# Attention and two mixture layers on one core: maxima over partitions by TensorE products instead of GpSimd's all-reduce, mask and identity by VectorE instead of GpSimd's select

## The chip, the cores and the metric

The kernel runs on one core of a Trainium2 chip. The time is device microseconds (us) of one execution, from its first to its last instruction and the little that lies around them; a comparison takes the median of several executions of each kernel on the same chip. A core has five engines with a queue of their own, each worked off in order: TensorE (PE, with its weight loads, PEld), VectorE (DVE), ScalarE (ACT), GpSimd (POOL) and SyncE (SP, which issues the transfers).

## The reference

Three layers follow each other; the inputs of the second layer's weights are float64, all others float32.

```python
# 1. attention, q, k, v: (2, 8, 576, 64); sm_attn: softmax(q k^T / 8) v
out_d = sm_attn(mean4(q), mean4(k), mean4(v))       # 144 pooled positions
out_up = np.repeat(out_d, 4, axis=2)
scores = np.where(np.abs(i - j) < 4, q @ k.T / 8, -1e9)
x = out_up + softmax(scores) @ v                    # -> (1152, 512)
# 2. gated layer, w_gate, w_val: (512, 1536), w_out: (1536, 512)
g = x @ w_gate
x = (g * sigmoid(g) * (x @ w_val)) @ w_out
# 3. eight experts, w1: (8, 512, 1024), w2: (8, 1024, 512)
logits = x @ w_gate2
P = np.exp(logits - logits.max())
for _ in range(8):
    P /= P.sum(1, keepdims=True) + 1e-09
    P /= P.sum(0, keepdims=True) + 1e-09
    P *= N / E
out = sum(P[:, e:e+1] * (np.maximum(x @ w1[e], 0) @ w2[e]) for e in range(8))
```

## The kernel before, in words

**Attention.** The 16 heads go in 8 pairs. Of a pair, `pooled` (L326) adds groups of four columns: k on VectorE (`kd`), q on GpSimd (`qt`, `qd`), and `pooled_v` (L338) the same of v on GpSimd (`vt`, `vdz`). `scores` (L347) puts the mask into PSUM by a product of `identb` and `maskb` (L352), adds q k^T for five windows of 128 keys (L355, L359) and the pooled scores (L361); VectorE takes the maxima (`stm`, `nb`), ScalarE the exponentials (`ex`), and GpSimd divides by the sums (L384 to L388). `turn` (L391) transposes the result on TensorE with `ident` (L397 to L401), and `combine` (L408) multiplies by v (L417, L425). In the same time the first column blocks of the second layer are made ready and multiplied.

**Second layer.** The weights come as words of float64, are put together into float32 by ACT and DVE (`load_f64`, L162, tiles `raw` and `cv`), and split into a high and a low half of 16 bits (`split`, L143): ACT writes the high half (L147), DVE the low one (L148). A product is three products of halves (`mm3`, L150, all on L155). The halves need a scale, a power of two from the largest magnitude of the operand: per partition from an ACT or DVE pass, then over the partitions by `allmax` (L138), then four DVE instructions on a column (`pow2`, L129 to L132: `u`, `u`, `s`, `i`). There are twelve column blocks f; tokens go in two chunks c, of 512 (c = 0) and 640 (c = 1). `prep_gv` makes block f ready, `gv_step` multiplies it (`gv`), and chunk 1 follows chunk 0 by three blocks. Blocks 0 to 2 of chunk 0 run beside the attention.

**Third layer.** The operands of the seven products of Winograd's form of Strassen's method (`p`, `h_step` L671), then the second product (`y`, `y_step` L721), for one expert after the other; weights come by `prep_w1` and `prep_w2`. The routing (`routing`, L596) has eight iterations: row sums on DVE (`rs`), and a product of `ones` and `prob` on TensorE (L612) for column sums, read by DVE (`cs`, L613 to L617).

**What sets the order.** Each engine's queue is laid down in advance by a scheduler that simulates the program; the code's own order, priorities and waits are its input. In the queue nothing overtakes.

**Where `allmax` is used.** 34 places: the bound on x1 (`v`), the twelve blocks (`gv`), two chunks of the second layer's product (`a`), two of its output (`x2`), the logits (`lg`), and `w1` and `w2` of eight experts. Before, it is one GpSimd instruction,

```python
        G.partition_all_reduce(g, mx, channels=P, reduce_op=RED.max)      # L140
```

one to twelve columns wide; where there is more than one column, the caller reduces them by DVE behind it. The mask of the band, the identity and `ones` are made at the start by GpSimd (L98 to L117); ACT copies `ident` to `identb` and `mask` to `maskb`.

Of the kernel before, what the change touches and what calls it, by code (L numbers as in the profile page):

```python
# [8 lines left out]
F32 = mybir.dt.float32  # L9
F16 = mybir.dt.float16  # L10
BF16 = mybir.dt.bfloat16
# [5 lines left out]
RED = bass_isa.ReduceOp  # L17
# [38 lines left out]
def tile_kernel(ctx, tc, qT, kT, vw, vd4, va, wgv, wo, wg2, w1, w2, out):  # L56
# [14 lines left out]

    def tmp(n, nm):
        return wp.tile([P, 16], F32, tag="tmp", bufs=56, name=nm)[:, :n]

# [1 line left out]
    # products of zeros while the first loads run, so that the tensor engine's clock is up  # L76
# [10 lines left out]
    V.memset(qz[0][64:, 0], 0.0)  # L87
    V.memset(qz[0][:64, 1], 0.0)
    V.memset(qz[1][64:, 0], 0.0)
# [3 lines left out]
    for i in range(2):  # L93
# [3 lines left out]
    mask = ap.tile([P, P], F32, tag="mask", bufs=1, name="mask")  # L97
    G.memset(mask, 0.0)  # L98
    G.affine_select(out=mask, in_=mask, compare_op=ALU.is_ge, fill=NEG, base=FAC - 1,
                    pattern=[[-1, P]], channel_multiplier=1)  # L100
    band = G.affine_select(out=mask, in_=mask, compare_op=ALU.is_ge, fill=NEG, base=FAC - 1,
                    pattern=[[1, P]], channel_multiplier=-1)
    with tc.issue_after(band.ins):
        ident = ap.tile([P, P], F32, tag="ident", bufs=1, name="ident")
        make_identity(nc, ident)
        identb = ap.tile([P, P], BF16, tag="identb", bufs=1, name="identb")
        A.copy(identb, ident)
        maskb = ap.tile([P, 4, P], BF16, tag="maskb", bufs=1, name="maskb")
        A.copy(maskb, mask[:, None, :].to_broadcast([P, 4, P]))
        G.memset(qz[1][:64, 1], 0.0)  # L110
        for i in range(2):
            G.memset(vz[i][:, :, 0, 64:], 0.0)
            G.memset(vz[i][:, :, 1, :64], 0.0)
            G.memset(vdz[i][:, :, 0, 64:], 0.0)
            G.memset(vdz[i][:, :, 1, :64], 0.0)
        ones = cp.tile([P, P], F32, name="ones")
        G.memset(ones, 1.0)  # L117
# [20 lines left out]
    def allmax(mx, n, nm):  # L138
        g = tmp(n, f"g_{nm}")
        G.partition_all_reduce(g, mx, channels=P, reduce_op=RED.max)  # L140
        return g
# [20 lines left out]
    def load_f64(src, nm, relu):  # L162
        """float64 words -> float32, by moving sign, exponent and mantissa.

        The high words, read as float32, order like the float64s; up to HI_MIN lie magnitudes below float32's
        normal range, whose exponents must not wrap: they become zeros."""
        raw = wp.tile([P, 2 * DM, 2], U32, tag="raw", bufs=2, name=f"raw{nm}")
        nc.sync.dma_start(raw.rearrange("p n w -> p (n w)"), src.bitcast(U32))
        f = mp.tile([P, 2 * DM], F32, tag="cv", bufs=2, name=f"cv{nm}")
        o, lo, hi = f.bitcast(U32), raw[:, :, 0], raw[:, :, 1]  # L170
        h = hi.bitcast(F32)
        if relu:
            A.activation(f, h, AF.Relu, scale=-1.0)
# [38 lines left out]
    def prep_w1(e):  # L212
        """The left operands of the seven products, of one column block of each half at a time."""
# [8 lines left out]
        m = tmp(1, f"mw1{e}")  # L222
        V.tensor_reduce(m, allmax(mx, 4, f"w1{e}"), axis=AX.X, op=ALU.max)
        s, inv = pow2(m, 1, f"w1{e}", room=4.0)
# [25 lines left out]
    def prep_w2(e):  # L250
# [10 lines left out]
        m = tmp(1, f"mw2{e}")  # L261
        V.tensor_reduce(m, allmax(mx, 4, f"w2{e}"), axis=AX.X, op=ALU.max)
        s, inv = pow2(m, 1, f"w2{e}")
# [55 lines left out]
    def attention():  # L319
        """Generator: the pieces of the attention, of two heads at a time."""  # L320
# [153 lines left out]
    def gv_step(c, f, early):  # L474
# [17 lines left out]
        if early:  # L492
            # silu(g) = g (1 + tanh(g / 2)) / 2, in the table that holds exp
# [30 lines left out]
    def act_split(c):  # L524
# [3 lines left out]
        g = allmax(sc, KF1, f"a{c}")  # L528
        m = tmp(1, f"ma{c}")
        V.tensor_reduce(m, g, axis=AX.X, op=ALU.max)  # L530
        s, ia[c] = pow2(m, 1, f"a{c}")
# [16 lines left out]
    def w_out(c):  # L548
        """x2, its part of the routing's logits, and the right operands of the seven products."""
# [18 lines left out]
    def operands(c, x2, mx):  # L568
        o, nh = CH[c]
        pool = m2 if c else mp  # L570
        m = tmp(1, f"m2{c}")
        V.tensor_reduce(m, allmax(mx, KD, f"x2{c}"), axis=AX.X, op=ALU.max)
        s, ix2[c] = pow2(m, 1, f"x2{c}", room=4.0)
# [22 lines left out]
    def routing():  # L596
# [4 lines left out]
        g = allmax(m, 1, "lg")  # L601
        V.tensor_scalar(g, g, -1.0, None, op0=ALU.mult)
# [3 lines left out]
        for it in range(8):  # L606
# [4 lines left out]
            ps = psr.tile([P, 512], F32, tag="rt", name=f"cs{it}")  # L611
# [37 lines left out]
    psr = ctx.enter_context(tc.tile_pool(name="psr", bufs=1, space=PSUM, reuse_waits="tile"))  # L649
    psm = ctxP.enter_context(tc.tile_pool(name="psm", bufs=2, space=PSUM, reuse_waits="tile"))  # L650
# [9 lines left out]
    lgps = psr.tile([P, 512], F32, tag="rt", name="lgps")[:, :TT * KD * E]  # L660
    lgps = lgps.rearrange("p (t d e) -> p t d e", t=TT, d=KD)
# [9 lines left out]
    def h_step(e, c, between=None):  # L671
        """relu(w1^T x2) by Winograd's form of Strassen's seven products, on halves of rows, columns and k."""
# [141 lines left out]
```

## Time and profile before

| | us |
|---|---|
| median of 3 runs | 1089.38 |
| lowest and highest | 1088.95, 1089.58 |
| span of the profiled execution | 1088.1 |
| PE busy in it | 1022.6 (94%) |
| DVE, ACT, POOL busy | 763.4, 449.8, 96.7 |
| mean granted clock of TensorE | 0.975 |

The span of the profiled execution runs from its first to its last instruction; the median of the runs is 1.3 us above it. The profile's page gives busy time by engine and, in forty slices of 27.2 us, the busy share in tenths. Granted clock 1.00 is TensorE's full speed (2.4 GHz), 0.5 its lower level (1.2 GHz). The attention fills the first 176 us; from there on TensorE works almost without a gap.

### The profile page before, as it was taken

The page shows a single profiled execution, that of the slowest core. Times are in us where ns is not written, and L with a number is a line of the kernel's source. Part 1 is how long each engine was busy: PE and PEld are TensorE (multiplying, and loading weights), DVE is VectorE, ACT ScalarE, POOL GpSimd, SP SyncE. Part 2 cuts the span into 40 slices and gives each one's busy share as a digit, 9 for nine tenths or more (in the row PEclk, how much of TensorE's full clock was granted, in tenths as well). Part 3 has the DMA queues.
Part 4 walks back from the last instruction along what each step waited for, and adds up shares of the span by engine and source line. Part 5 has one row for each costly group of instructions (what it writes and reads, how often), then busy time and mean ns, then how long its engine had stood idle before and what let it go on. Part 6 is the DMA issues. An engine that isn't in the chain of part 4 may idle for free.

```text
span 1088.1 us, 16397 instructions
## 1 busy us (share of the span) xinstructions
PE 1022.6 (94%) x6493; PEld 657.3 (60%) x6493; DVE 763.4 (70%) x1557; ACT 449.8 (41%) x933; POOL 96.7 (9%) x147
## 2 busy tenths in 40 slices
PE   5756677999999999999999999999999999999998
PEld 4745455566656776656666565575665665666654
DVE  5835565788768299979758866984974974985631
ACT  4654364666646073723414422621541441351210
POOL 3634440000000020000000000000000000000000
PEclk9977888999999999999999999999999999999999
DMA  7721222243202002210301201211111030120001
GB/s 200 243 68 33 85 91 78 86 147 116 79 1 78 1 2 78 78 42 37 117 1 39 86 31 39 78 40 39 65 52 33 8 117 1 40 78 1 1 35 53
DMA packets 23613, 67.92 MB, mean 62 GB/s; under 512 B 12208, under 2 KB 12464, under 8 KB 17136
## 3 DMA queue, kind: packets, MB, share of 16 engines
q1 hardware_dynamic: 23536, 66.87, 18.2%
q8 instruction: 51, 0.84, 0.3%
q14 instruction: 26, 0.21, 0.1%
HBM read 64.50 MB, written 2.36 MB: 61 GB/s over the span
## 4 chain that ended last, share of the span: by engine, by line
PE 83%; DVE 6%; issue 6%; POOL 2%; ACT 2%; POOLq 0%; ACTq 0%; DVEq 0%
PE y L155 34%; PE p L155 29%; PE gv L155 9%; PE wo L155 6%; PE o L425 1%; PE lgps L546 1%; PE s L355 1%; PE s L361 0%; DVE nb L370 0%; DVE cvg L174 0%; ACT ex L373 0%; POOL ex L384 0%; DVE gv L148 0%; DVE stm L365 0%; POOL g_gv L140 0%
## 5 line engine op out<-in xcount | busy, mean ns | idle before, releaser
L155 PE MATMUL y<-w,hhl 128*128 128x512 f16 (+1 forms) x1752 | 396.2, 376 | 0.0
L155 PE MATMUL p<-bop,w 128*128 128x320 f16 (+1 forms) x2688 | 353.8, 286 | 0.8 <-DVE u L685 0.7
L155 PEld LDWEIGHTS <-w 128*128 128x128 f16 x2688 | 263.0, 98 | 90.5 <-issue 1.3
L155 PEld LDWEIGHTS <-hhl 128*128 128x128 f16 x1752 | 171.5, 98 | 178.0
L155 PE MATMUL gv<-xhl,gv 128*128 128x320 f16 (+1 forms) x864 | 148.9, 333 | 5.7 <-DVE act L504 4.0
L713 ACT ACTIVATE hhl<-h 128x640 f16<-128x640 f32 (+1 forms) x128 | 83.1, 676 | 169.0 <-DVE h L685 169.0
L155 PEld LDWEIGHTS <-gv 128*128 128x128 f16 x864 | 85.5, 99 | 63.1 <-issue 12.5
L744 DVE SCALAR_TENSOR_TENSOR acc<-y,pe,acc 128x512 f32<-128x512 f32 (+1 forms) x64 | 47.3, 739 | 101.3 <-PE y L155 100.5
L147 ACT ACTIVATE w<-r,s_w 128x256 f16<-128x256 f32 (+1 forms) x96 | 71.0, 783 | 110.2 <-PE y L155 86.3
L714 DVE SCALAR_TENSOR_TENSOR hhl<-h,hhl 128x640 f16<-128x640 f32 (+1 forms) x128 | 94.3, 753 | 15.9 <-ACT hhl L713 14.7
L685 DVE SCALAR_TENSOR_TENSOR h<-p,u 128x256 f32<-128x256 f32 (+1 forms) x192 | 84.8, 452 | 19.0 <-PE p L155 13.3
L148 DVE SCALAR_TENSOR_TENSOR w<-r,s_w,w 128x256 f16<-128x256 f32 (+1 forms) x96 | 78.2, 833 | 16.7 <-ACT w L147 16.7
L155 PE MATMUL wo<-ahl,wo 128*128 128x320 f16 (+1 forms) x432 | 71.5, 326 | 0.0
L685 DVE SCALAR_TENSOR_TENSOR u<-p,u 128x320 f32<-128x320 f32 (+1 forms) x128 | 57.3, 448 | 4.8 <-PE p L155 4.1
L147 ACT ACTIVATE w<-cmb,s_w 128x512 f16<-128x512 f32 x64 | 43.0, 710 | 41.1 <-DVE cmb L238 38.9
L155 PEld LDWEIGHTS <-wo 128*128 128x128 f16 x432 | 42.3, 99 | 26.9
L140 POOL PARTITION_ALL_REDUCE g_w<-mxw x16 | 7.3, 458 | 567.1 <-DVE mxw L136 331.8
L702 ACT ACTIVATE s<-p 128x256 f32<-128x256 f32 (+1 forms) x64 | 25.4, 397 | 53.3 <-PE p L155 53.3
L136 DVE TENSOR_REDUCE mxw<-r 128x1 f32<-128x1024 f32 x32 | 37.5, 1213 | 14.1 <-DMA r<-in_w 14.1
L148 DVE SCALAR_TENSOR_TENSOR w<-cmb,s_w,w 128x512 f16<-128x512 f32 x64 | 45.9, 741 | 0.0
L258 ACT ACTIVATE j<-r 128x1024 f16<-128x1024 f32 x32 | 33.4, 1046 | 25.4 <-DMA r<-in_w 25.4
L373 ACT ACTIVATE ex<-s,nb 128x128 f32<-128x128 f32 x64 | 22.6, 372 | 24.7 <-DVE nb L367 24.2
(192 smaller groups left out, 956.2 us busy)
## 6 DMA issues: line engine op xcount, KB each, us to landing
r<-in_w SPq DMA_DIRECT2D x32, 1024.0 KB, 4.8
rawg<-in_wgv SPq DMA_DIRECT2D x12, 1024.0 KB, 5.1
rawo<-in_wo SPq DMA_DIRECT2D x6, 1024.0 KB, 4.9
vz<-in_vw SPq DMA_DIRECT2D x16, 160.0 KB, 4.6
k<-in_kT SPq DMA_DIRECT2D x8, 288.0 KB, 6.7
qz<-in_qT SPq DMA_DIRECT2D x16, 144.0 KB, 4.0
v<-in_vd SPq DMA_DIRECT2D x8, 288.0 KB
va<-in_va SPq DMA_DIRECT2D x8, 288.0 KB, 7.9
```

The lines of the kernel that those rows point to most:

```text
L136: V.tensor_reduce(o, i, axis=axis, op=ALU.max, apply_absolute_value=True)
L147: return (A.activation(hi, src, AF.Copy, scale=s), V.scalar_tensor_tensor(lo, src, s, hi, op0=ALU.mult, op1=ALU.subtract))
L148: V.scalar_tensor_tensor(lo, src, s, hi, op0=ALU.mult, op1=ALU.subtract))
L155: T.matmul(ps, lhsT=wf(i, k), rhs=xf(j, k), start=n == 0, stop=n == 3 * nk - 1)
L258: A.activation(junk, t[:, 2 * j:2 * j + 2].rearrange("p a n -> p (a n)"), AF.Abs, accum_out=mx[:, 2 * i + j:2 * i + j + 1])
L355: T.matmul(ps[0][:, w * P:(w + 1) * P], lhsT=q[:, j, ws], rhs=k[:, ws], start=False, stop=w == NW - 2)
L373: A.activation(ex[:, 0, w * P:(w + 1) * P], ps[0][:, w * P:(w + 1) * P], AF.Exp, scale=0.125, bias=nb[:, w:w + 1], accum_out=sm[:, w:w + 1])
L685: V.scalar_tensor_tensor(o, ps, HSC, u, op0=ALU.mult, op1=ALU.add)
L702: A.activation(s1, p1, AF.Copy, scale=HSC)
L713: ra = A.activation(t[:, 0], h, AF.Relu)
L714: rv = V.scalar_tensor_tensor(t[:, 1], h, 0.0, t[:, 0], op0=ALU.max, op1=ALU.subtract)
L744: V.scalar_tensor_tensor(acc[t][:, ds], ps, p[:, t:t + 1], acc[t][:, ds], op0=ALU.mult, op1=ALU.add)
```

## The change

`allmax` becomes: a DVE maximum over the columns where there are several, a product with the identity that turns the column into a row in one partition of PSUM, a DVE maximum along that row, and a product of a row of ones with the one number, which puts it into all partitions; the four instructions of `pow2` read it in PSUM. The piece of PSUM comes from `small`: during the attention a buffer of the two that the early blocks' `gv` products use (tag `y`), afterwards one tile `rt` that lives to the end, whose bank also holds the logits and the routing's column sums. The mask and the identity come from arithmetic on a table of column minus row that DVE builds. GpSimd clears the `qz` tiles. Comments went too; lines move by up to 11.

```diff
+    def small(nm):
+        if routed:
+            return routed[0][:, TT * KD * E:]
+        return psg.tile([P, 512], F32, tag="y", name=f"sm_{nm}")
...
-    mask = ap.tile([P, P], F32, tag="mask", bufs=1, name="mask")
-    G.memset(mask, 0.0)
-    G.affine_select(out=mask, in_=mask, compare_op=ALU.is_ge, fill=NEG, base=FAC - 1,
-                    pattern=[[-1, P]], channel_multiplier=1)
...
-        make_identity(nc, ident)
-        A.copy(identb, ident)
-        A.copy(maskb, mask[:, None, :].to_broadcast([P, 4, P]))
...
+    V.memset(dist[:, 0:1], 0.0)
+    for n in (1, 2, 4, 8, 16, 32, 64):
+        V.tensor_scalar(dist[:, n:2 * n], dist[:, :n], float(n), None, op0=ALU.add)
+    V.transpose(row, dist[:, :32])
+    for n in range(32, P, 32):
+        V.tensor_scalar(row[n:n + 32, 0:1], row[n:n + 32, 0:1], float(n), None, op0=ALU.add)
+    V.tensor_scalar(dist, dist, row[:, 0:1], None, op0=ALU.subtract)
+    V.tensor_tensor(dist, dist, dist, op=ALU.mult)
+    V.tensor_scalar(identb, dist, 0.0, None, op0=ALU.is_equal)
+    V.tensor_scalar(maskb, dist[:, None, :].to_broadcast([P, 4, P]), FAC * FAC - 0.5, NEG,
+                    op0=ALU.is_ge, op1=ALU.mult)
+    V.tensor_scalar(ident, dist, 0.0, None, op0=ALU.is_equal)
...
     def allmax(mx, n, nm):
-        g = tmp(n, f"g_{nm}")
-        G.partition_all_reduce(g, mx, channels=P, reduce_op=RED.max)
-        return g
+        if n > 1:
+            m = tmp(1, f"gm_{nm}")
+            V.tensor_reduce(m, mx, axis=AX.X, op=ALU.max)
+            mx = m
+        ps = small(nm)
+        r = tmp(1, f"gr_{nm}")
+        T.matmul(ps[:1, :P], lhsT=mx, rhs=ident, start=True, stop=True)
+        V.tensor_reduce(r[:1], ps[:1, :P], axis=AX.X, op=ALU.max)
+        T.matmul(ps[:, P:P + 1], lhsT=ones[:1], rhs=r[:1], start=True, stop=True)
+        return ps[:, P:P + 1]
...
-            ps = psr.tile([P, 512], F32, tag="rt", name=f"cs{it}")
+            ps = routed[0]
```

The order of POOL's queue in the attention, third pair's scaling (`ex`) and fifth pair's sums. `ISA` stands for a custom instruction: of each two rows of L140 the first sets up the engine's code and the second is the all-reduce, and the one of L334 sets it up again for the ordinary operations. Before:

```order
L384 TENSOR_TENSOR ex_606<-ex_606,rs_614 128x512
L386 TENSOR_SCALAR ex_606<-ex_606,rs_614 128x128
L388 TENSOR_TENSOR ex_606<-ex_606,rs_614 72x288
L140 ISA
L140 ISA g_gv_479<-mxg_477 128x1
L334 ISA
L334 TENSOR_TENSOR qd_827<-qt_830 128x288
```

and now:

```order
L399 TENSOR_TENSOR ex_617<-ex_617,rs_625 128x512
L401 TENSOR_SCALAR ex_617<-ex_617,rs_625 128x128
L403 TENSOR_TENSOR ex_617<-ex_617,rs_625 72x288
L360 TENSOR_TENSOR vdz_85<-vt_955 72x2x64
L348 TENSOR_TENSOR qt_978<-qz_81 128x576
```

No custom instruction stands between them any more; over the whole queue one is left, ahead of the first `vt`.

The order of PE's queue where block 6 of the second layer begins (`mxg`: a block's maxima by partition, `gr`: the number, `gv_1639` and `gv_1665`: block 6's weights). Before:

```order
L155 MATMUL gv_2_1_1834<-xhl,gv_1317 128x320
L155 LDWEIGHTS gv_1639
L155 MATMUL gv_6_0_1911<-xhl,gv_1639 128x512
L155 LDWEIGHTS gv_1639
L155 MATMUL gv_6_0_1911<-xhl,gv_1639 128x512
```

and now:

```order
L174 MATMUL gv_2_1_1864<-xhl,gv_1331 128x320
L157 MATMUL rt<-ident,mxg_1674 1x128
L159 MATMUL rt<-gr_gv_1676,ones 128x1
L157 MATMUL rt<-ident,mxg_1788 1x128
L159 MATMUL rt<-gr_gv_1790,ones 128x1
L174 LDWEIGHTS gv_1665
L174 MATMUL gv_6_0_1943<-xhl,gv_1665 128x512
```

The four products of blocks 6 and 7 stand directly ahead of the first product that needs block 6's scale; it is the same at blocks 10 and 11.

The order of PE's queue at the routing's fourth column sums, around the end of the first expert's `p` products and the start of its `y` products. Before:

```order
L155 MATMUL y_0_0_4305<-w_0_3_3958,hhl_0_7_3908 128x512
L612 MATMUL cs_3636<-prob,ones 128x72
L155 LDWEIGHTS hhl_0_2_3831
L155 MATMUL y_1_0_4332<-w_0_1_3952,hhl_0_2_3831 128x512
```

and now:

```order
L174 MATMUL p_1_27_4263<-bop_3550,w_0_11_2984 128x320
L622 MATMUL rt<-prob,ones 128x72 x5
L157 MATMUL rt<-ident,gm_w_3980 1x128
L159 MATMUL rt<-gr_w_3982,ones 128x1
L174 LDWEIGHTS hhl_0_0_3625
L174 MATMUL y_0_0_4351<-w_0_0_3993,hhl_0_0_3625 128x512
```

Before, the eight column sums lie among products, 50 to 120 `p` or `y` products apart, and the `y` products begin while `p` products are left. Now the first three are spread, and the last five follow each other without a product between them, with the two of `w2`'s maximum behind them and the first `y` product, which needs the scale from it, behind those. On DVE the reduces and divisions of these iterations follow each other in the same way.

## Rows read from the trace of the kernel before

**Rows 1.** The page: busy time by engine; PE's busy tenths and the granted clock in tenths, both in 40 slices of 27.2 us; and one of the costliest groups, with busy us and mean ns.

```profile
PE 1022.6 (94%) x6493; PEld 657.3 (60%) x6493; DVE 763.4 (70%) x1557; ACT 449.8 (41%) x933; POOL 96.7 (9%) x147
...
PE   5756677999999999999999999999999999999998
...
PEclk9977888999999999999999999999999999999999
...
L714 DVE SCALAR_TENSOR_TENSOR hhl<-h,hhl 128x640 f16<-128x640 f32 (+1 forms) x128 | 94.3, 753 | 15.9 <-ACT hhl L713 14.7
```

**Rows 2.** Busy time by stretch: start:end, length, then PE, PEld, DVE, ACT, POOL busy (instructions), granted clock, the transfers' busy share and GB/s.

```profile
0.00:176.00 176.00, 114.92 (x740) 93.73 (x741) 102.79 (x228) 85.95 (x320) 75.70 (x115) 0.84 0.38 111
13.50:49.00 35.50, 32.51 (x251) 30.25 (x252) 29.44 (x65) 23.84 (x114) 24.14 (x35) 0.95 0.76 233
49.00:176.00 127.00, 80.10 (x486) 62.91 (x485) 67.22 (x150) 59.92 (x204) 48.10 (x64) 0.80 0.22 65
405.00:430.00 25.00, 25.00 (x168) 16.33 (x166) 24.76 (x59) 11.94 (x20) 0.39 (x1) 1.00 0.25 85
488.60:576.40 87.80, 87.80 (x554) 54.03 (x553) 64.83 (x126) 31.59 (x53) 0.74 (x2) 1.00 0.14 49
```

**Rows 3.** The chain of waits that ended last: first its shares in 45 to 180 us (135 us), then pieces of it in order of time (start, length, what). "issue" is time in which the engine waited for nothing the profile shows. The row at 52.73 is the longest such piece; 49.37 and 162.60 are the first and the last of eleven such pieces of over 1 us, 43.8 us together, that lie at GpSimd's all-reduces.

```profile
by line: issue 37.8%; PE o L425 6.2%; PE gv L155 5.1%; DVE nb L370 3.6%; POOL ex L384 3.1%; PE o L417 2.4%; DVE stm L365 2.3%; PE s L361 2.2%; ACT ex L373 2.2%; POOL qd L334 2.1%; DVE cvg L174 1.7%; DVE cvg L179 1.7%; POOL qt L333 1.7%; DVE
...
49.37 2.91 issue
...
52.73 8.64 issue
...
162.60 5.53 issue
...
176.31 3.88 PE gv L155 x18
```

**Rows 4.** GpSimd in order of time: start, length, line, operation; in brackets the idle time before it and what ended it.

```profile
10.37 0.28 POOL L99 TENSOR_SCALAR_AFFINE_SELECT mask<-mask 128x128 f32<-128x128 f32 x1 [9.45 <-issue]
...
52.28 0.38 POOL L140 PARTITION_ALL_REDUCE g_v<-mxv  x1 [6.34 <-issue]
...
61.37 1.14 POOL L333 TENSOR_TENSOR qt<-qz 128x576 f32<-128x576 f32 x1 [8.71 <-issue]
...
76.36 0.38 POOL L140 PARTITION_ALL_REDUCE g_gv<-mxg  x1 [5.97 <-issue]
...
83.58 0.65 POOL L334 TENSOR_TENSOR qd<-qt 128x288 f32<-128x288 f32 x1 [6.84 <-issue]
```

**Rows 5.** Who waited for whom in 13.5 to 176 us: total us, times, longest.

```profile
DVE u_gv L129 <- POOL g_gv L140: 35.1, 5, 9.6
...
PE s L352 <- ACT identb L107: 10.0, 1, 10.0
```

**Rows 6.** TensorE, transposes of a head's scores (`turn`), four to a row: the first head, the fourth, the sixteenth and last.

```profile
25.81 0.60 PE L397 MATMUL t<-ident,ex 128*128 128x128 f32 x4
...
38.80 0.60 PE L397 MATMUL t<-ident,ex 128*128 128x128 f32 x4
...
161.69 0.60 PE L397 MATMUL t<-ident,ex 128*128 128x128 f32 x4
```

**Rows 7.** The chain of waits at the routing: TensorE's smallest float32 products, the logits' with 8 columns (three products) and column sums with 72 (one product). A float32 product is two records.

```profile
382.52 0.57 PE lgps L546 x6
...
410.36 0.17 PE cs L612 x2
```

**Rows 8.** TensorE in order of time, 36 to 45 us: start, length (the last one's modelled end included), records. L359 is one float32 product of 128 columns; the eight records of L355 stand there twice, behind work and behind a gap.

```profile
36.62 1.05 PE L355 MATMUL s<-k,qz 128*128 128x128 f32 x8
...
38.04 0.44 PE L359 MATMUL s<-k,qz 128*128 128x128 f32 x2
38.32 0.65 PE L309 MATMUL vv<-va 128*128 128x128 bf16 x5
...
42.74 0.47 PE L352 MATMUL s<-maskb,identb 128*128 128x512 bf16 x1 [2.98 <-DVE x L431]
43.00 1.91 PE L355 MATMUL s<-k,qz 128*128 128x128 f32 x8
```

**Rows 9.** VectorE in order of time: the first and the last of five small instructions of one routing iteration that follow each other.

```profile
407.02 0.22 DVE L617 TENSOR_TENSOR prob<-prob,cs 128x72 f32<-128x72 f32 x1
...
408.00 0.23 DVE L610 TENSOR_TENSOR prob<-prob,rs 128x72 f32<-128x72 f32 x1
```

**Rows 10.** VectorE, one instruction of `pow2` over the third layer: 15 of them, busy us, mean ns.

```profile
L129 DVE TENSOR_SCALAR u_w<-mw 128x1 f32<-128x1 f32 x15 | 2.2, 149 | 0.2
```

**Rows 11.** The split of a block's 1024 columns in order of time: the high half on ACT, the low one (of a later block) on DVE.

```profile
191.08 1.13 ACT L147 ACTIVATE gv<-cvg,s_gv 128x1024 f16<-128x1024 f32 x1
...
208.02 1.28 DVE L148 SCALAR_TENSOR_TENSOR gv<-cvg,s_gv,gv 128x1024 f16<-128x1024 f32 x1 [1.21 <-ACT gv L147]
```

**Rows 12.** The tail of a block of the second layer: ACT's pass over `gv`, DVE's `act`.

```profile
184.83 0.79 ACT L514 ACTIVATE act<-gv,iv 128x640 f32<-128x640 f32 x1 [1.18 <-PE gv L155]
...
188.14 0.88 DVE L515 SCALAR_TENSOR_TENSOR act<-gv,iv,act 128x640 f32<-128x640 f32 x1 [5.25 <-issue]
```

**Rows 13.** VectorE, the same instruction of four columns, alone and while GpSimd works.

```profile
22.85 0.15 DVE L370 TENSOR_TENSOR nb<-stm,scl 128x4 f32<-128x4 f32 x1
...
66.51 2.95 DVE L370 TENSOR_TENSOR nb<-stm,scl 128x4 f32<-128x4 f32 x1
```

More of the change, by code (lines that the diff above doesn't have):

```diff
@@ L4 @@
 import concourse.tile as tile
-from concourse import bass_isa, mybir
+from concourse import mybir
 from concourse._compat import with_exitstack
-from concourse.masks import make_identity
 F32 = mybir.dt.float32
@@ L16 @@
 PSUM = bass.MemoryType.PSUM
-RED = bass_isa.ReduceOp
 B, H, S, D = 2, 8, 576, 64
@@ L70, in ps_mm @@
         return psm.tile([P, 2, 512], F32, tag="mm", name=nm)
+    def small(nm):
+        if routed:
+            return routed[0][:, TT * KD * E:]
+        return psg.tile([P, 512], F32, tag="y", name=f"sm_{nm}")
+    routed = []
     def tmp(n, nm):
@@ L86, in tile_kernel @@
     sts = [ap.tile([P, 8], F32, tag=f"sts{i}", bufs=1, name=f"sts{i}") for i in range(2)]
-    V.memset(qz[0][64:, 0], 0.0)
-    V.memset(qz[0][:64, 1], 0.0)
-    V.memset(qz[1][64:, 0], 0.0)
+    for i in range(2):
+        G.memset(qz[i][64:, 0], 0.0)
+        G.memset(qz[i][:64, 1], 0.0)
     scl = ap.tile([P, 8], F32, tag="scl", bufs=1, name="scl")
@@ L95, in tile_kernel @@
         V.memset(sts[i], 1.0)
-    mask = ap.tile([P, P], F32, tag="mask", bufs=1, name="mask")
-    G.memset(mask, 0.0)
-    G.affine_select(out=mask, in_=mask, compare_op=ALU.is_ge, fill=NEG, base=FAC - 1,
-                    pattern=[[-1, P]], channel_multiplier=1)
[L101 to L104, printed above, removed]
-        make_identity(nc, ident)
-        identb = ap.tile([P, P], BF16, tag="identb", bufs=1, name="identb")
-        A.copy(identb, ident)
-        maskb = ap.tile([P, 4, P], BF16, tag="maskb", bufs=1, name="maskb")
-        A.copy(maskb, mask[:, None, :].to_broadcast([P, 4, P]))
[L110 to L117, printed above, removed]
+    for i in range(2):
+        G.memset(vz[i][:, :, 0, 64:], 0.0)
+        G.memset(vz[i][:, :, 1, :64], 0.0)
+        G.memset(vdz[i][:, :, 0, 64:], 0.0)
+        G.memset(vdz[i][:, :, 1, :64], 0.0)
@@ new lines, in tile_kernel @@
+    ones = cp.tile([P, P], F32, name="ones")
+    G.memset(ones, 1.0)
+    dist = ap.tile([P, P], F32, tag="dist", bufs=1, name="dist")
+    V.memset(dist[:, 0:1], 0.0)
+    for n in (1, 2, 4, 8, 16, 32, 64):
+        V.tensor_scalar(dist[:, n:2 * n], dist[:, :n], float(n), None, op0=ALU.add)
+    row = ap.tile([P, 32], F32, tag="row", bufs=1, name="row")
+    V.transpose(row, dist[:, :32])
+    for n in range(32, P, 32):
+        V.tensor_scalar(row[n:n + 32, 0:1], row[n:n + 32, 0:1], float(n), None, op0=ALU.add)
@@ new lines, in tile_kernel @@
+    V.tensor_scalar(dist, dist, row[:, 0:1], None, op0=ALU.subtract)
+    V.tensor_tensor(dist, dist, dist, op=ALU.mult)
+    identb = ap.tile([P, P], BF16, tag="identb", bufs=1, name="identb")
+    V.tensor_scalar(identb, dist, 0.0, None, op0=ALU.is_equal)
+    maskb = ap.tile([P, 4, P], BF16, tag="maskb", bufs=1, name="maskb")
+    V.tensor_scalar(maskb, dist[:, None, :].to_broadcast([P, 4, P]), FAC * FAC - 0.5, NEG,
+                    op0=ALU.is_ge, op1=ALU.mult)
+    ident = cp.tile([P, P], F32, name="ident")
@@ L221, in prep_w1 @@
             r.append(t)
-        m = tmp(1, f"mw1{e}")
-        V.tensor_reduce(m, allmax(mx, 4, f"w1{e}"), axis=AX.X, op=ALU.max)
-        s, inv = pow2(m, 1, f"w1{e}", room=4.0)
+        s, inv = pow2(allmax(mx, 4, f"w1{e}"), 1, f"w1{e}", room=4.0)
         a = []
@@ L260, in prep_w2 @@
             r.append(t)
-        m = tmp(1, f"mw2{e}")
-        V.tensor_reduce(m, allmax(mx, 4, f"w2{e}"), axis=AX.X, op=ALU.max)
-        s, inv = pow2(m, 1, f"w2{e}")
+        s, inv = pow2(allmax(mx, 4, f"w2{e}"), 1, f"w2{e}")
         b = []
@@ L527, in act_split @@
         V.tensor_tensor(sc, amx[c], wo_inv, op=ALU.mult)
[L528 to L531, printed above, removed]
+        s, ia[c] = pow2(allmax(sc, KF1, f"a{c}"), 1, f"a{c}")
         V.tensor_scalar(sc, wo_inv, s, None, op0=ALU.mult)
@@ L570, in operands @@
         pool = m2 if c else mp
-        m = tmp(1, f"m2{c}")
-        V.tensor_reduce(m, allmax(mx, KD, f"x2{c}"), axis=AX.X, op=ALU.max)
-        s, ix2[c] = pow2(m, 1, f"x2{c}", room=4.0)
+        s, ix2[c] = pow2(allmax(mx, KD, f"x2{c}"), 1, f"x2{c}", room=4.0)
         w = xp.tile([P, 7, 2, 2, nh], F16, tag=f"bop{c}", name=f"bop{c}")
@@ L600, in routing @@
         V.tensor_reduce(m, lg, axis=AX.XY, op=ALU.max)
-        g = allmax(m, 1, "lg")
-        V.tensor_scalar(g, g, -1.0, None, op0=ALU.mult)
+        g = tmp(1, "lgn")
+        V.tensor_scalar(g, allmax(m, 1, "lg"), -1.0, None, op0=ALU.mult)
         A.activation(prob, lg, AF.Exp, bias=g)
@@ L649, in tile_kernel @@
     psr = ctx.enter_context(tc.tile_pool(name="psr", bufs=1, space=PSUM, reuse_waits="tile"))
+    routed.append(psr.tile([P, 512], F32, name="rt"))
     psm = ctxP.enter_context(tc.tile_pool(name="psm", bufs=2, space=PSUM, reuse_waits="tile"))
@@ L659, in tile_kernel @@
     nc.sync.dma_start(wg2r, wg2)
-    lgps = psr.tile([P, 512], F32, tag="rt", name="lgps")[:, :TT * KD * E]
-    lgps = lgps.rearrange("p (t d e) -> p t d e", t=TT, d=KD)
+    lgps = routed[0][:, :TT * KD * E].rearrange("p (t d e) -> p t d e", t=TT, d=KD)
     for p in operands(0, *w_out(0)):
```

## The prediction

> **What bounds the kernel now.** I read the page first, then stretches, the chain of waits, GpSimd's rows, and who waits for whom. The page's slices [rows 1] show two parts: in the first six or seven PE is busy five to seven tenths at a granted clock below full; behind them it is full. By stretches [rows 2] PE is busy 114.9 of the first 176 us at clock 0.84, and 87.80 of 87.80 in the first expert's period measured. So a microsecond less of waiting counts in the attention, and a microsecond of additional TensorE work or waiting counts everywhere behind it. The dense part begins at 176.15 (the chain's last row starts at 176.31 with products without a gap [rows 3]).
>
> In the attention the chain is 37.8% of 135 us "issue", which is 51.0 us [rows 3]; the eleven pieces at the all-reduces make 43.8 of them. GpSimd's rows say what they are [rows 4]: an all-reduce takes 0.38 us, but the engine stands still for 6.34 and 5.97 us ahead of it, and for 8.71 and 6.84 ahead of the ordinary instruction behind it. The change from one kind of code to the other costs, not the maximum. DVE's scale waits 35.1 us in five goes for it [rows 5], and `qd` and the scaling stand behind it in GpSimd's queue. In the dense part blocks are made ready far ahead, and no such standstill is on the chain.
>
> **What goes in the attention.** The order leaves one custom instruction, ahead of the first `vt`, so all eleven standstills on the chain go. What is late next? Three ways:
> - By subtraction: 176.2 − 43.8 = 132.4, or 125.2 if all 51.0 go.
> - The start: the first scores waited 10.0 us for `identb` [rows 5], behind the 9.45 us that GpSimd stood still [rows 4]. DVE builds it now from some twenty small instructions of 0.15 to 0.25 us [rows 9, 10], 3 to 5 us, beside the first loads. I take 2.5 us earlier; the bounds are 0 and 4. It makes the two ends 129.9 and 122.7.
> - By DVE, the busiest engine beside PE: 29.44 + 67.22 = 96.7 us from 13.5 to 176 [rows 2]. In 13.5 to 49, with hardly a standstill, it was busy 29.44 of 35.50, 83%. From 11 at that pace it needs 116.5 us and ends at 127.5; at 95% it ends at 113.
> - By heads: first to fourth transposes took 13.0 us [rows 6], 4.3 a head; first to last 135.9, 9.1 a head. Less 43.8 the latter is 6.1 a head. The lower one leaves out the blocks' preparation that the others contain.
>
> I take 124, with 115 and 137 as bounds: 52 us earlier.
>
> **What is given back on TensorE.** Behind the attention PE has no gap, so what is added there counts in full.
> - Products moved: two pieces of block 2, 24 products, stood inside the attention and stand behind its last `combine` now. At 3.88 / 18 = 0.216 us [rows 3] it is 5.2 us, and 0.5 for a `y` buffer that the maxima share with them: 5.7.
> - The products of `allmax`: a float32 product of 128 columns starts its successor 0.28 us later [rows 8], one of few columns 0.17 to 0.19 [rows 7]; together 0.44. Of the 34 maxima the order has five inside the attention; of the 29 behind it five lie in the stalls below and are counted there: 24 × 0.44 = 10.6 us.
> - Blocks 6 and 10: their four small products stand directly ahead of the first product that needs their scale, and what stands behind them waits too. From the last product before: ACT's pass 0.79 and DVE's `act` 0.88 stand ahead in the queues [rows 12], then DVE's maximum of the row 0.25, the second product 0.19, four of `pow2` at 0.15 [rows 10], ACT's high half 1.13, and DVE's low half 1.28, of which PE's first products cover some 0.9 [rows 11]. That is 4.2 us, with the hand-overs between engines 4.8. Behind 2.98 us of idling the same eight products took 1.91 instead of 1.05 us [rows 8], which is the lower level of the clock; I put 2 us to each stall for it. Two stalls: 13.6; block 5, half covered: 1.
> - The routing: five column sums stand in a row, then `w2`'s maximum, then the first `y` product. Small DVE instructions follow each other every 0.245 us [rows 9]. An iteration is nine of them, 2.2 us, a product of 0.17 and two hand-overs: 2.6. Ahead of the first of the five DVE has the last `h` (about 0.45), two low halves of 0.753 [rows 1] and four steps of the row sums, 2.9 us; four iterations make 10.4; then reduce, product, `prob`, four `pe` and `pow2` 2.5; the high half 1.1; the low one partly covered, 0.6: 17.5 us, and 2.5 for the clock, 20. The stretch 405 to 430 shows what waits beside it: PE 25.00 of 25.00, DVE 24.76 [rows 2], so nothing else covers it.
>
> Sum: 5.7 + 10.6 + 13.6 + 1 + 20 = 50.9. GpSimd's later all-reduces save nothing, since nothing on the chain waits for them. DVE gets one small reduce more per maximum (34 × 0.25 = 8.5 us), of which those behind the attention lie in its idle 23 us per expert [rows 2].
>
> Bounds: a stall is between 3 and 7 us at each block, between 8 (the iterations covered by other work) and 26 (another half of queue ahead, DVE at 0.45 us a step) at the routing. The give-back lies between 34 and 62.
>
> The dense part of 911.95 us (176.15 to 1088.1) is kept: 124 + 912 + 51 = 1087 for the span; the median of the runs lies 1.3 above it. I forecast 1087, since the start's upper bound and the pace by heads pull the sum down by about as much. This is 0.2% below the median before, so gain and give-back cancel almost.
>
> The Trainium skill, "PSUM — Partial Sum Buffer", section on bank collisions, asks to guard PSUM by bank and quadrant, not by address. `rt`'s maximum columns lie beside the column sums in one bank, and the order has them one behind the other; no run here shows a collision. By it the routing's 20 us stand; by address alone `w2`'s two products could go ahead of the iterations, and the sum would be about 15 less.
>
> **Rivals.**
> - Faster: the heads go at 4.3 to 5.5 us and attention ends at 112 to 116; or the iterations hide. For it speaks the reload-free stretch [rows 6]; against it that DVE was 83% busy there [rows 2]. 124 − 10 and stalls 6 less: 1071.
> - Slower: DVE becomes the attention's bound, slowed by GpSimd that now never pauses. The same four-column instruction took 0.15 us alone and 2.95 beside GpSimd's scaling [rows 13]. 16 heads at 7 us and its ends give 25.8 + 105 + 9 = 140 for attention's end: 140 + 912 + 51 + 1 = 1104. It decides from an end of 128 on, where gain (48) falls below the give-back.
> - The change doesn't do what it says: the standstills belong to GpSimd's ordinary instructions, and remain. Then only the give-back is left: 1089 + 51 = 1140. Against it: the order shows no second custom instruction. By the Trainium skill, "GPSIMD Engine Reference", section 4.1 (Engine selection), a reduction along the partitions belongs on GpSimd. Taken alone the rule would lead here; the trace agrees in the dense part (0.38 us, nobody waiting) and disagrees in the attention, by the standstills.
>
> **How the numbers follow.** Within 0.2% (2.2 us) is what a measurement of this kernel can't tell from no change. Forecast 0.46 (own range 1078 to 1097; faster 0.21, same 0.15, slower 0.10); faster rival 0.25; slower rival 0.26 (0.03 of it same); nothing gained 0.03. So faster 0.46, same 0.18, slower 0.36. Range: to the faster rival's end and the slower rival's middle, 1069 to 1106; it leaves out some 0.1 above and 0.1 below.
>
> **What would show it.** No "issue" of over 5 us on GpSimd behind 20 us; dense products from 115 to 137; PE gaps of 3 to 7 us in front of blocks 6 and 10, one chain of DVE and PE at the routing of 15 to 20 us with PE idle and a granted clock below 1.00 behind it; an expert's period of 88.7 (87.8 and two maxima of 0.44). Wrong would be: an attention end past 137 with DVE near full, or a routing gap below 8 us.

## The result, and the profile after

The changed kernel takes 1100.22 us (median of 4 runs, 1097.35 to 1102.93), the kernel before 1089.16 (1088.03 to 1089.58): ratio 1.0104, 95% interval 1.0085 to 1.0122. It is slower by 11 us. The time lies in the range of the prediction, on the side of its slower chances; the forecast, 1087, was 13 us too low.

The page of the changed kernel, beside [rows 1] (the same lines; slices of 27.5 us). The line numbers are those of the changed kernel from here on, up to 19 above those of before: the products of halves, L155 before, are L174 now, and the two products of `allmax` are L157 and L159. The runs below have numbers of their own again.

```profile
PE 1049.2 (96%) x6629; PEld 662.0 (60%) x6629; DVE 785.1 (71%) x1605; ACT 449.0 (41%) x931; POOL 82.6 (8%) x111
...
PE   5788999989999968999999999999999999999998
...
PEclk9898998999999987999999999999999999999999
```

The first slices are fuller (5, 7, 8, 8, 9 for 5, 7, 5, 6, 6) at a clock that is higher on the whole (0.95 beside 0.84 in the next rows). Behind them stand dips that were not there before: PE's 6 and 8 and the clock's 8 and 7 in the fifteenth and sixteenth slice (384 to 439 us), the clock's 8 in the seventh (165 to 192), and PE's 8 in the ninth (220 to 247). By stretches, beside [rows 2]:

```profile
0.00:126.20 126.20, 101.77 (x738) 86.05 (x739) 98.36 (x232) 80.87 (x311) 77.05 (x107) 0.95 0.55 147
49.00:126.20 77.20, 68.63 (x520) 59.59 (x519) 60.93 (x141) 58.02 (x212) 48.88 (x61) 0.96 0.31 86
400.00:420.00 20.00, 6.08 (x25) 3.82 (x24) 14.54 (x65) 3.06 (x4) 0.00 (x0) 0.60 0.00 0
420.00:440.00 20.00, 19.69 (x83) 8.17 (x82) 13.17 (x17) 4.33 (x6) 0.00 (x0) 0.88 0.28 106
593.51:682.95 89.44, 89.44 (x562) 54.44 (x562) 66.10 (x129) 30.80 (x52) 0.00 (x0) 1.00 0.14 48
```

The attention takes 126.2 us instead of 176, with PE busy 101.8 of them at clock 0.95, not 114.9 of 176 at 0.84. Between 400 and 420 PE is busy 6.08 us, and an expert's period is 89.44 us where it was 87.80. Both halves of the change are there at once: 50 us won, 60 given back. From the start of the dense part to the end it is 1098.5 − 126.2 = 972.3 us, before 911.95. The 126.2 is one execution: the first five runs below have the same order of TensorE's queue in the attention, and in their profiles the same products behind it start at 122.4 to 127.6.

The attention's marks on TensorE, beside [rows 6] and the last of [rows 3] (start, length; in brackets the idle time before it and what ended it):

```profile
11.25 0.59 PE L367 MATMUL s<-maskb,identb 128*128 128x512 bf16 x1 [7.75 <-DVE maskb L125]
...
22.74 0.60 PE L412 MATMUL t<-ident,ex 128*128 128x128 f32 x4
...
119.59 0.60 PE L412 MATMUL t<-ident,ex 128*128 128x128 f32 x4
...
126.16 5.34 PE L174 MATMUL gv<-xhl,gv 128*128 128x512 f16 x24
```

The first scores start at 11.25 instead of 13.52. First to last transposes take 96.9 us for fifteen heads, 6.5 each, where they took 9.1. On GpSimd no standstill like those of [rows 4] is left, in which it waits for nothing ("issue"); behind its first clearing it waits for other engines and transfers only, as here:

```profile
35.52 0.72 POOL L356 TENSOR_TENSOR vt<-v 72x256 f32<-72x256 f32 x1 [7.16 <-DMA v<-in_vd]
...
105.32 0.45 POOL L360 TENSOR_TENSOR vdz<-vt 72x128 f32<-72x128 f32 x1 [5.37 <-PE o L432]
```

The first piece that was given back, ahead of block 6 (TensorE, in order of time):

```profile
169.71 0.38 PE L157 MATMUL rt<-ident,mxg 128*1 128x128 f32 x2
171.02 0.38 PE L159 MATMUL rt<-gr_gv,ones 1*128 1x1 f32 x2 [0.93 <-DVE gr_gv L158]
172.73 0.59 PE L157 MATMUL rt<-ident,mxg 128*1 128x128 f32 x2 [1.33 <-ACT gv L208]
173.69 0.58 PE L159 MATMUL rt<-gr_gv,ones 1*128 1x1 f32 x2 [0.37 <-DVE gr_gv L158]
174.21 2.31 PE L174 MATMUL gv<-xhl,gv 128*128 128x512 f16 x5
```

The `gv` products stop at 169.71 and go on at 174.21. Of the four small products the third waits longest, 1.33 us, for ACT's pass over block 7, whose scale nobody needs yet; it stands ahead of block 6's products in the queue. The second, at the routing:

```profile
397.75 3.42 PE L174 MATMUL p<-bop,w 128*128 128x320 f16 x24
403.53 0.44 PE L622 MATMUL rt<-prob,ones 128*128 128x72 f32 x2 [2.35 <-DVE prob L620]
406.31 0.70 PE L622 MATMUL rt<-prob,ones 128*128 128x72 f32 x2 [2.34 <-DVE prob L620]
409.25 0.70 PE L622 MATMUL rt<-prob,ones 128*128 128x72 f32 x2 [2.23 <-DVE prob L620]
...
415.11 0.70 PE L622 MATMUL rt<-prob,ones 128*128 128x72 f32 x2 [2.23 <-DVE prob L620]
416.14 0.58 PE L157 MATMUL rt<-ident,gm_w 128*1 128x128 f32 x2 [0.32 <-DVE cs L623]
417.09 0.58 PE L159 MATMUL rt<-gr_w,ones 1*128 1x1 f32 x2 [0.37 <-DVE gr_w L158]
419.50 1.01 PE L174 MATMUL y<-w,hhl 128*128 128x512 f16 x2 [1.83 <-ACT w L166]
```

From the last `p` products' end at 401.2 to the first `y` at 419.50 nothing but column sums and the maximum of `w2` runs, and each sum waits 2.2 to 2.4 us for DVE's nine small instructions. One iteration takes 2.94 us (409.25 less 406.31).

### The profile page after: what moved, and what is told of

It is laid out like the page before. It is cut to its first block, busy times and chain, and to the rows that moved or that the text cites. A ratio compares the mean times of both kernels' runs of the same rounds, so it can differ in the third digit from the quotient of the medians.

```text
span 1098.5 us, 16633 instructions
## 1 busy us (share of the span) xinstructions
PE 1049.2 (96%) x6629; PEld 662.0 (60%) x6629; DVE 785.1 (71%) x1605; ACT 449.0 (41%) x931; POOL 82.6 (8%) x111
## 4 chain that ended last, share of the span: by engine, by line
PE 86%; DVE 6%; ACT 3%; DMA 3%; issue 1%; SPq 0%; POOL 0%; DVEq 0%; ACTq 0%
PE y L174 34%; PE p L174 29%; PE gv L174 11%; PE wo L174 7%; DMA rawg<-in_wgv 1%; ACT ex L388 1%; DMA va<-in_va 1%; PE o L440 1%; PE rt L157 1%; PE rt L558 1%; PE rt L159 1%; DMA v<-in_vd 1%; PE o L432 0%; DVE gv L167 0%; DMA qz<-in_qT 0%
## 5 line engine op out<-in xcount | busy, mean ns | idle before, releaser
L174 PE MATMUL y<-w,hhl 128*128 128x512 f16 (+1 forms) x1752 | 392.2, 378 | 2.1 <-ACT w L166 1.8
L174 PE MATMUL p<-bop,w 128*128 128x320 f16 (+1 forms) x2688 | 350.3, 286 | 0.0
L174 PEld LDWEIGHTS <-w 128*128 128x128 f16 x2688 | 261.2, 98 | 84.7 <-issue 1.8
L174 PEld LDWEIGHTS <-hhl 128*128 128x128 f16 x1752 | 171.8, 98 | 189.1 <-issue 7.1
L174 PE MATMUL gv<-xhl,gv 128*128 128x320 f16 (+1 forms) x864 | 148.6, 331 | 1.4 <-DVE gv L167 0.6
L174 PEld LDWEIGHTS <-gv 128*128 128x128 f16 x864 | 84.1, 99 | 58.8 <-issue 7.3
L174 PE MATMUL wo<-ahl,wo 128*128 128x320 f16 (+1 forms) x432 | 73.6, 330 | 0.0
L695 DVE SCALAR_TENSOR_TENSOR u<-p,u 128x320 f32<-128x320 f32 (+1 forms) x128 | 57.5, 449 | 7.7 <-PE p L174 7.6
L174 PEld LDWEIGHTS <-wo 128*128 128x128 f16 x432 | 42.3, 100 | 27.9 <-issue 0.9
L712 ACT ACTIVATE s<-p 128x256 f32<-128x256 f32 (+1 forms) x64 | 25.5, 399 | 60.9 <-PE p L174 60.9
L695 DVE SCALAR_TENSOR_TENSOR u<-p,s 128x256 f32<-128x256 f32 (+1 forms) x64 | 28.9, 452 | 9.9 <-PE p L174 8.6
L695 DVE SCALAR_TENSOR_TENSOR h<-p,s 128x256 f32<-128x256 f32 (+1 forms) x64 | 28.9, 452 | 5.8 <-PE p L174 5.8
```

What stands on the lines that cost most here:

```text
L695: V.scalar_tensor_tensor(o, ps, HSC, u, op0=ALU.mult, op1=ALU.add)
L712: A.activation(s1, p1, AF.Copy, scale=HSC)
```

## The experiments

The runs are counted in the order in which they were made (the label's number). All times are medians of four runs or more, beside runs of the kernel before on the same chip (1089.2 to 1089.8); ratios are to it.

**The two halves apart.** The first run keeps the new maxima in the attention and goes back to GpSimd behind it; `routed` is the list that is filled when the attention's pools close.

```diff
     def allmax(mx, n, nm):
...
+        if routed:
+            g = tmp(1, f"g_{nm}")
+            G.partition_all_reduce(g, mx, channels=P, reduce_op=RED.max)
+            return g
         ps = small(nm)
```

> The changed kernel with the 28 maxima behind the attention on GpSimd again (the six up to block 4 stay on TensorE). My theory: the attention still ends at about 126 us, and the dense part falls back to 912 us plus the 24 moved products (5.2 us): span about 1044, time about 1046, ratio to the kernel before 0.960. Rival: the dense part starts 50 us earlier than its weights and splits can be made ready, so part of the attention's gain comes back as waits for block 5 and later whatever computes the maxima: 1060 to 1075. A second rival, that the attention itself gains little without the rest, would give 1085 or more.

Measured: 1046.16 us, ratio 0.9592 (0.9574 to 0.9611), 4% faster than the kernel before. The theory's figure was met, and both rivals fall: the dense part keeps up with a start some 50 us earlier. An expert's period there is the old one:

```profile
500.00:587.80 87.80, 87.80 (x555) 54.02 (x553) 65.08 (x127) 30.89 (x53) 0.70 (x2) 1.00 0.14 49
```

The other half, `if not routed:` in the same place:

> The other half: the six maxima up to block 4 on GpSimd, the 28 behind the attention on TensorE. My theory, that the two halves add up: the difference of the changed kernel to the first run (1100.2 less 1046.2 is 54.0), less some 5 because the 24 products stay inside the attention, on the kernel before: 1138 to 1143. Rival: the standstills in the attention would partly go by the other edits (mask, earlier start): below 1130.

Measured: 1147.26, ratio 1.0525 (1.0509 to 1.0540). It is 4 us above the theory's upper figure, and the rival falls. The halves are −43.1 and +57.5 us, which makes +14.4; together they are +11.0. They add up to within 3.4 us. Both halves contain the new mask, which alone costs 5.2 us in the eighth run (below), where TensorE's queue in the attention has the same order as in this run; counted once, the halves make +9.2. The moved products are in the first half alone: in this run the 24 stay inside the attention, as before.

**The routing.** One maximum of 34 on GpSimd:

```diff
+        if nm == "w20":
+            g = tmp(1, f"g_{nm}")
+            G.partition_all_reduce(g, mx, channels=P, reduce_op=RED.max)
+            return g
```

> The changed kernel with one of the 34 maxima, that of w2 of expert 0, on GpSimd. My theory: the standstill at the routing (PE busy 6.1 of 400 to 420 us) stands there because the first y products wait for a scale whose two products stand behind the eight column sums in the one PSUM tile. Freed of it the y products come between the sums: 18 to 22 us less, time about 1080. Rival: the sums themselves are late (DVE), and the y products would wait for something else: within 3 us of 1100.

Measured: 1091.14, ratio 1.0016 (1.0003 to 1.0029): 9 us less than the changed kernel, half of what the theory said, and more than the rival's 0 to 3. Where the rest stayed, TensorE's rows of this run show:

```profile
447.28 0.38 PE L164 MATMUL rt<-gr_w,ones 1*128 1x1 f32 x2 [0.37 <-DVE gr_w L163]
...
452.10 5.77 PE L179 MATMUL p<-bop,w 128*128 128x256 f16 x30 [4.44 <-ACT w L171]
...
458.46 0.82 PE L179 MATMUL p<-bop,w 128*128 128x256 f16 x6 [0.59 <-ACT s L717]
...
461.46 2.13 PE L179 MATMUL p<-bop,w 128*128 128x256 f16 x18 [2.18 <-DVE u L700]
```

The standstill at 401 is gone, and a new one stands at 447 to 461: it is the next maximum in the tile, that of `w1` of expert 1, whose products now stand behind the column sums. This speaks for the tile and not for `w2`: whatever maximum comes next stands behind the sums. The fifth run tests it and gives the maxima a bank of their own:

```diff
-KB = 5
+KB = 4
...
-            return routed[0][:, TT * KD * E:]
+            return routed[1]
...
     routed.append(psr.tile([P, 512], F32, name="rt"))
+    routed.append(psr.tile([P, 512], F32, name="sm"))
```

> The changed kernel with a PSUM bank of its own for the maxima's products, apart from the one of the logits and column sums; it is taken from the pool of the expert products (KB 4 instead of 5). All 34 maxima stay on TensorE. My theory: the standstill at the routing comes from the shared tile alone, which keeps the maximum of w2 behind the eight sums; it goes, and with the two block standstills left the time is 1080 to 1083, plus what a fifth buffer is worth (0 to 5 us, to be read from an expert's period against 89.44). Rival: a maximum behind a sum is late whatever tile it has, because DVE works the iterations off first: the standstill stays or moves to another maximum, 1092 to 1100.

Measured: 1081.12, ratio 0.9913 (0.9896 to 0.9931), 19 us less than the changed kernel, as the theory said; the rival falls. The period stays 89.44, so the lost buffer costs nothing there, and the stretch that was empty is full:

```profile
400.00:420.00 20.00, 20.00 (x109) 10.52 (x108) 16.78 (x41) 5.03 (x9) 0.00 (x0) 1.00 0.23 83
```

**The blocks.**

```diff
+        if routed and nm[:2] == "gv":
+            g = tmp(1, f"g_{nm}")
+            G.partition_all_reduce(g, mx, channels=P, reduce_op=RED.max)
+            return g
```

> The changed kernel with the maxima of blocks 5 to 11 of the second layer on GpSimd, all others on TensorE. My theory: the two standstills ahead of blocks 6 and 10 (about 5 us each with the clock behind them) go, and three further pairs of products at 0.82: about 12 us less, time about 1088. Rival: the splits (ACT, DVE) are late there in any case, and the block waits as long: within 3 us of 1100.

Measured: 1082.92, ratio 0.9932 (0.9913 to 0.9951), 17 us less than the changed kernel, 5 more than expected; the rival falls. The blocks' stage alone: from the dense `gv` products (behind the 0.52 us wait for `act` in both) to the first `wo` product it is 112.25 us (148.89 to 261.14) where the changed kernel takes 127.47 (147.45 to 274.92), 15.2 less (the other 2 us lie outside this stage and were not followed). Of that three pairs of products at 0.82 (below) are 2.5, so the two standstills with the lower clock behind them, and block 5's wait of 0.36, are 12.7, some 6.2 a standstill.

**What one maximum costs.** The first run with the maxima of experts 1 to 7 on TensorE again:

```diff
-        if routed:
+        if routed and not (nm[0] == "w" and nm[2] != "0"):
```

> As the first, but the 14 maxima of experts 1 to 7 (w1 and w2) on TensorE. They stand among dense products with no gap, so the difference to the first run is 14 times what one maximum costs PE. By the trace of the changed kernel a period grew by 1.64 us for two, so 0.82 each: 11.5 us more than the first run. By the prediction's 0.44 each: 6.2 us more. If the longer period had another cause than the two products: 0.

Measured: 1065.55, ratio 0.9786 (0.9755 to 0.9817), 19.4 us above the first run instead of 11.5. The period is 89.44 against 87.80, so 0.82 a maximum is right, and 0.44 is wrong; what the total has more is a standstill of `w1`'s maximum behind the column sums, as in the third run (PE busy 16.75 of the 23 us from 427 on; the first run has no such gaps around its column sums). Why 0.82? TensorE and its weight loads in this run, around the two products of one maximum:

```profile
648.64 0.38 PE L162 MATMUL rt<-ident,gm_w 128*1 128x128 f32 x2
648.95 0.39 PE L179 MATMUL y<-w,hhl 128*128 128x512 f16 x1
...
654.16 0.38 PE L164 MATMUL rt<-gr_w,ones 1*128 1x1 f32 x2
654.47 2.62 PE L179 MATMUL p<-bop,w 128*128 128x320 f16 x18
```

and the weight loads:

```profile
648.64 0.09 PEld L162 LDWEIGHTS rt<-ident,gm_w 128*1 128x1 f32 x2 [0.26 <-issue]
648.95 0.10 PEld L179 LDWEIGHTS <-hhl 128*128 128x128 f16 x1 [0.22 <-issue]
...
654.16 0.29 PEld L164 LDWEIGHTS rt<-gr_w,ones 1*128 1x128 f32 x2 [0.26 <-issue]
654.47 1.61 PEld L179 LDWEIGHTS <-w 128*128 128x128 f16 x13
```

From its start to the next product's it is 0.31 us each time; the other 0.10 of 0.41 is, by subtraction, its own late start. The weight loads stand still for 0.26 us ahead of the small product's and 0.22 behind it: a load comes at its product, and not during the one before it. 128*1 and 1*128 in the rows are the tile of the array that a product uses. Not every shape other than 128*128 does this. In the attention of the changed kernel tiles of 72*72 and 72*128 stand between full ones, products and then weight loads:

```profile
116.82 0.41 PE L416 MATMUL t<-ident,ex 72*72 72x72 f32 x4
117.07 1.32 PE L440 MATMUL o<-at,vz 128*128 128x124 f32 x10
118.23 0.66 PE L432 MATMUL o<-at,vdz 72*128 72x144 f32 x4
...
116.71 0.35 PEld L416 LDWEIGHTS t<-ident,ex 72*72 72x72 f32 x4
117.01 1.19 PEld L440 LDWEIGHTS o<-at,vz 128*128 128x128 f32 x10
118.13 0.55 PEld L432 LDWEIGHTS o<-at,vdz 72*128 72x128 f32 x4
```

Each of these loads begins 0.06 to 0.11 us ahead of its product, and no idle time stands before it. The ninth run makes a maximum one product of full shape, by giving the column as 128 equal weight columns:

```diff
-        T.matmul(ps[:1, :P], lhsT=mx, rhs=ident, start=True, stop=True)
-        V.tensor_reduce(r[:1], ps[:1, :P], axis=AX.X, op=ALU.max)
-        T.matmul(ps[:, P:P + 1], lhsT=ones[:1], rhs=r[:1], start=True, stop=True)
-        return ps[:, P:P + 1]
+        T.matmul(ps[:, :P], lhsT=mx.to_broadcast([P, P]), rhs=ident, start=True, stop=True)
+        V.tensor_reduce(r, ps[:, :P], axis=AX.X, op=ALU.max)
+        return r
```

> As the second run (experts 1 to 7 on TensorE, blocks and the rest behind the attention on GpSimd), but a maximum is one product instead of two: the column is given as 128 equal weight columns, so that each partition of PSUM gets the whole row, and one DVE maximum along it ends in all partitions. The second run's period was 89.44 against the first run's 87.80: 0.82 for two products, 0.41 each, while a column sum of the routing costs 0.17 to its successor's start. My theory: what a small product costs is its odd shape, 128*1 or 1*128, ahead of and behind which the weight loads stand still (0.22 to 0.26 us each); at full shape they are loaded ahead, so one product costs about 0.28: period 88.36, time about 1057 to 1060 (the wait for the column sums stays). Rival: the change to float32 and back costs 0.41 whatever the shape: period 88.62.

Measured: 1051.76, ratio 0.9651 (0.9630 to 0.9672), 13.8 us below the second run. The period is 88.22 (724.05 less 635.83): 0.21 a maximum, below both figures. Seven periods at 1.22 less are 8.5 of the 13.8 us; the attention, too, is shorter, which the theory had not (the products behind it start at 117.56 instead of 124.82). Its rows:

```profile
635.83 0.38 PE L162 MATMUL rt<-ident,gm_w 128*128 128x128 f32 x2
636.05 0.38 PE L178 MATMUL y<-w,hhl 128*128 128x512 f16 x1
```

and the weight loads:

```profile
635.70 0.33 PEld L162 LDWEIGHTS rt<-ident,gm_w 128*128 128x128 f32 x2
635.94 0.10 PEld L178 LDWEIGHTS <-hhl 128*128 128x128 f16 x1
```

The weight load runs ahead again, without an idle gap, and the next product starts 0.22 us later. The rival, 0.41 whatever the shape, falls: a full product with 128 columns costs half of what one with a single weight column or a single weight row does.

The Trainium skill, "TensorEngine Tiling (Array Packing)", section Key Properties, says that changing the tiling mode drains TensorE. The rows with tiles of 128*1 and 1*128 fit it, with 0.41 against 0.21 us a product, and those with 72*72 and 72*128 show no such standstill; the mode itself is not in the trace, only the tile's shape, so no run shows that it is the reason.

**Mask and identity.** The first run with the old mask, and the kernel before with the new one (diffs as in the change, in one direction or the other):

> The first run (attention's maxima on TensorE, the others on GpSimd) with mask and identity made by GpSimd and ACT as before. First scores at 13.5 instead of 11.3 us: if that shift lasts, 1048.4. If the loads set the pace until 40 us, as the chain of the changed kernel says (it runs over transfers from 5.5 to 33 us), nothing: 1046. If GpSimd, late with its clearing, holds back v: up to 1051.

> The kernel before with mask and identity by VectorE, all 34 maxima on GpSimd. The same 2.2 us at the start: 1087 if they last; 1089 if the first all-reduce's standstill or the loads take them back.

Measured: 1046.58 (0.9601, 0.9587 to 0.9615) and 1094.90 (1.0044, 1.0027 to 1.0060). In the faster frame the new mask is worth nothing, as its second figure said. Alone it is 5 us slower, which neither of its figures said: the last products of the attention with 120 columns start 3.9 us later than before (178.52 against 174.62), with the same all-reduces and standstills at other places. In both comparisons the scheduler has laid TensorE's queue in the attention in another order, so neither shows what the mask is worth in an unchanged order; why the order of the eighth run is the worse one stays open.

**Versions that beat both.** The first run with the one full product, and all 34 maxima on TensorE with the bank of its own and the full product:

> The first run (attention's maxima on TensorE, the rest on GpSimd) with the one full product. Six maxima, on PE 0.5 us each less and a hand-over between engines less: if the attention is bound by DVE, nothing beyond 1 us of 1046; if its pace hangs on the maxima, up to 5 less.

> All 34 maxima on TensorE, as in the changed kernel, with the bank of its own (1081 us) and the one full product. 24 maxima at 0.28 instead of 0.82: 13 less; the two block standstills, with a product and a hand-over less per maximum, 1 to 2 less each: 1064 to 1068. By the rival, a product costing 0.41 whatever its shape: 24 times 0.41 less, 1071.

Measured: 1040.49 (0.9553, 0.9537 to 0.9569) and 1058.07 (0.9710, 0.9696 to 0.9725). The first is the fastest of all, 4.5% below the kernel before; it gains 5.7 us, somewhat more than its upper figure, and the attention's last combine in it starts its last products at 116.55 instead of 121.29. It need not be the hand-over that is saved: with the one product the scheduler lays TensorE's queue in the attention in another order, the same in the ninth, tenth and eleventh runs. In these three the products behind the attention start at 117.6 to 119.3, in the changed kernel and the first five runs, with the old order, at 122.4 to 127.6. Hand-over and order were not taken apart. The second is what the change itself comes to without its two flaws: 3% faster instead of 1% slower. It is 6 us better than expected, since a full product is 0.21 and not 0.28 (1.7 us for 24), and the attention is shorter there as well (118.19 for the same products, 124.11 in the fifth run). The standstills at blocks 6 and 10 are still in it.

## Why the prediction was wrong, step by step

The range held the time, the sign did not: the forecast and the larger chance were on faster. The mechanism was right, with what is won and what is given back in the places that were named; the size of one term was wrong.

- Attention: right. Its end was put at 124 with bounds 115 and 137; it is 126.2, and 122.4 to 127.6 in the five runs with the same order, so the 2.2 us lie within what executions differ by. The first scores start at 11.25, put at 11; heads take 6.5 us, put at 6.1. The standstills at the all-reduces went. (Of the eleven pieces in the sum one, 1.19 us at 111.95, lies within GpSimd's ordinary scaling; the other ten make 42.6.) The faster rival (4.3 to 5.5 us a head, an end at 112 to 116) and the slower one (7 us a head, an end at 140) both fall; DVE, the slower one's bound, is busy 60.9 of the last 77.2 us, 79%.
- Moved products: right, 24 in 5.3 us behind the last combine (126.16 to 131.44), put at 5.2.
- The products of `allmax`: this step failed. It took 0.44 for a maximum, "a float32 product of 128 columns starts its successor 0.28 us later [rows 8], one of few columns 0.17 to 0.19 [rows 7]". It measured 0.82, so 24 cost 19.7 us, not 10.6; the prediction's own sign, a period of 88.7, came out as 89.44. (The period measures 14 of the 24; the other ten, of the same two shapes, are taken at the same price.) The rows were well read, but they were of full products of 128*128; the new ones have tiles of 128*1 and 1*128, and the weight loads that the others hide come to light. The order rows ahead of the prediction show the shapes, `1x128` and `128x1`, and no row of before had one like them, so this price had to have bounds of its own; instead it had a value and none.
- Blocks 6 and 10: right in size, 12.7 us with the clock and block 5's wait, put at 13.6 and half of 1. The chain was a little different: what ACT had ahead of block 6's high half was the pass over block 7 (1.33 us of PE's wait), not one over the block before. Small waits at 135 and 147 us are 0.25 and 0.52.
- The routing: right in size, 19.1 us by the fifth run against 20. The iterations take 2.94 us, not 2.6: the sums themselves take 0.70 in place of 0.34 to 0.44 us, in a stretch with a granted clock of 0.60, and DVE waits 0.79 for each; what stands ahead of the first, 2.35 us of waiting behind the last product, is a little less.
- Sum: 5.3 + 19.7 + 12.7 + 0.8 + 19.1 = 57.6 of the 60.4 measured; 2.8 us are not assigned. With 126.2 in place of 124 and 19.7 in place of 10.6 the prediction's own sum is 1087 + 2.2 + 9.1 = 1098.3, and the span is 1098.5. That it meets to 0.2 us is luck: the other terms came out 2.4 us lower than they were put, and the 2.8 us that are not assigned make up for it. The change was near its point of balance, and one small price, 24 times, decided the sign.
- The rule on banks that was weighed (the Trainium skill, "PSUM — Partial Sum Buffer", section on bank collisions) is in agreement with the routing's queue, in which the shared bank's users keep their order; a bank of its own gives 19 us back (fifth run). That run gives the maxima another tile and another bank at once, so it doesn't show which of the two set the order. No run shows a collision.

## What to carry to other kernels

A reduction over partitions belongs where its latency is paid: here the maxima on GpSimd, with the swaps of its code, cost some 50 us while the engine had other work, and nothing that shows in an expert's period afterwards, so the best version uses TensorE in the first part and GpSimd in the second. A product that is put into a dense stream should not have a single weight column or row if it can have the full shape, and its price is read from start to start of its neighbours, weight loads included. A buffer that two chains share makes the order of one the order of the other: look in the queue for what stands ahead of the first user of a late value. Where a scheduler lays the queues, a small edit can reorder a whole stage: compare the queues before a difference is put down to the edit.

## What was not expected of the hardware

- A float32 product with one weight column or one weight row cost 0.41 us in a stream at full clock (0.82 for two, 89.44 less 87.80 for two maxima), a full one 0.21; the weight loads on both sides stood still for 0.22 to 0.26 us. Tiles of 72*72 and 72*128 between full ones showed no such standstill.
- GpSimd's standstills came on both sides of an all-reduce, 5.97 to 8.71 us [rows 4], where GpSimd has other work around it. The 28 all-reduces behind the attention in the first run cost nothing that shows (period 87.80, as before); GpSimd has only two pairs of ordinary instructions there, and what it waits for before each all-reduce is DVE or ACT.
